# Attention and feed-forward in one kernel: the projected K transposed by DMA, V projected onto both partition halves, and the first stages reordered

## Chip, cores, metric

One core of one Trainium2 chip. The metric is the device time of one execution in microseconds (us), given as the median of several. A profiled execution has a span (first to last instruction) about 1.8 us shorter than its device time (518.4 against 520.21 us before). Executions of one kernel here scatter by 0.4 to 5 us, which is as much as the effects under study, so below I also use an interval inside a profile that repeated to 0.01 us in three profiles of the change.

## The reference

```python
# q, k, v: (8 batches, 8 heads, 1024 tokens, 64); E, F: (64, 1024)
k_proj = np.einsum('ks,bhsd->bhkd', E, k)
v_proj = np.einsum('ks,bhsd->bhkd', F, v)
scores = np.matmul(q, k_proj.transpose(0, 1, 3, 2)) / np.sqrt(64)
attn = softmax(scores)                       # over the 64 projected keys
x = np.matmul(attn, v_proj)                  # -> (8192 tokens, 512)
h = np.maximum(x @ w_in, 0.0)                # w_in: 512 x 2048
out = h * h @ w_out                          # w_out: 2048 x 512, f32 out
```

## The kernel before

Everything runs in bf16 with f32 sums. GpSimd's queue loads and casts (f32 to bf16). TensorE's order is fixed by hand. The feed-forward part (FFN) of batch b goes in 64 numbered *steps*, each of four 128x512 matmuls (0.86 us), and `at(step, stage)` puts the attention stages of the next batches between them. Batches are counted from 0 here. "Second batch" is batch 1. LO and HI are partitions 0 to 63 and 64 to 127. A PSUM bank holds the sums of TensorE until another engine has copied them out. A *slot* is the time from the start of one matmul to the start of the next.

```python
def load(t, src):                         # all loads but E
    return nc.gpsimd.dma_start(t, src)
...
for g in range(2):                        # batch 0, in two halves of four heads
    load(K0[:, half[g]], tokens(k, 0, h=half[g]))
    load(Q0[:, half[g], 0:4, :], tokens(q, 0, h=half[g], i=slice(0, 4)))
    if g == 0:
        make_identity(nc, ident[:])
load(f_bf[:], F[:])
for g in range(2):
    load(V0[:, half[g]], tokens(v, 0, h=half[g]))
... # then w_in, w_out (with the second half of Q0 before its last piece), K, V, Q of batch 1, 2, ...

def project(self):                        # K and V of one batch, in pairs of matmuls
    ps = bank()                           # one of four PSUM banks, shared with the FFN
    for i in range(NI):
        nc.tensor.matmul(ps[LO, :], lhsT=ET[:, i, :], rhs=self.K[:, :, i, :], ...)
        nc.tensor.matmul(ps[HI, :], lhsT=FT[:, i, :], rhs=self.V[:, :, i, :], ...)
    self.keep_k(ps[LO, :])                # two VectorE copies 64x512 into kp
    self.keep_v(ps[HI, :])                # ScalarE and VectorE copies into both halves of vp

def transpose_k(self, h=slice(0, 8)):
    ps = bank([P, H, KP], BF16)
    for hh in range(h.start, h.stop):     # eight transposes, 64 rows -> 64 columns
        nc.tensor.transpose(ps[:, hh, :], self.kp[:, hh].rearrange("k a d -> k (a d)"), ident[0:KP, 0:KP])
    nc.vector.tensor_copy(self.kT[:, h], ps[:, h])

def transpose_q_dma(self):                # Q is transposed by DMA from batch 2 on
    nc.sync.dma_start_transpose(self.qT[...], self.Q[...])
... # plan
at(36, nxt.project); at(37, nxt.transpose_q, 0); at(37, nxt.transpose_q, 1)   # batch 1, during batch 0
at(61, coming.project); at(64, coming.transpose_k)                            # batch 2, during batch 0
at(30, coming.project); at(49, coming.transpose_k)                            # later batches
```

The softmax here doesn't subtract the row's maximum and nothing guards it: scores larger than these inputs give would overflow.

## Time and profile before

| | before |
|---|---|
| median (lowest to highest) | 519.8 us (519.7 to 520.09) |
| TensorE busy | 507.5 of 518.4 us |
| a batch in the steady part (same place, next batch) | 61.18 us |
| 128x512 matmuls, start to start | 0.216 us |

The page of the profile before: the span, busy time and share of each engine, then 40 slices of the span with busy tenths, granted TensorE clock in tenths and the share of the DMA engines.

```profile
span 518.4 us, 6881 instructions
...
PE 507.5 (98%) x2774; PEld 224.2 (43%) x2774; DVE 175.7 (34%) x369; ACT 286.1 (55%) x426; POOL 31.9 (6%) x44
...
PE   7899999999999999999999999999999999999997
...
PEclk8999999999999999999999999999999999999999
DMA  9999999899997299204831050110101011010102
```

TensorE has work in every slice; DMA is at nine tenths in thirteen of the first sixteen slices and falls away later. Whether those first slices are limited by one or the other cannot be read from shares, so next comes the chain of work that ended last in the profile before (start, duration, what).

```profile
14.31 16.57 DMA w_in_122<-in_moe_w_in_dram
31.17 30.68 DMA Q_sb<-in_q_dram
61.90 1.07 PE ps_bank L227 x16
```

The chain is a DMA chain until 61.9 us: the load of the second batch's Q, issued at 31.17 us behind megabytes of weights, K and V, lands at 61.85 us, and TensorE's transposes of it (L227) follow at once. From there on the chain is TensorE. The waits of TensorE before (who waited for what: us in total, times, longest):

```profile
PE ps_bank L328 <- DVE xT L311: 1.1, 2, 0.9
PE ps_bank L207 <- ACT kp L172: 0.8, 1, 0.8
PE ps_bank L183 <- ACT o_sb L341: 0.6, 1, 0.6
...
PE ps_bank L227 <- DMA Q_sb<-in_q_dram: 0.6, 1, 0.6
```

L227 waited 0.6 us for Q. So at that point TensorE was the earlier of the two, but only just.

Two places where K is transposed, from the timeline of TensorE before (start, duration, instruction, count). First the block at step 49 of a steady batch, then the one of the second batch:

```profile
140.89 1.03 PE L334 MATMUL ps_bank<-w_out_124,hsq 128*128 128x512 bf16 x4
141.85 0.41 PE L248 MATMUL ps_att<-expT,ones 64*64 64x512 bf16 x4
142.09 0.39 PE L282 MATMUL ps_att<-expT,vp 64*64 64x512 bf16 x4
142.41 0.40 PE L207 MATMUL ps_bank<-ident,kp 64*128 64x64 bf16 x8
142.75 1.04 PE L334 MATMUL ps_bank<-w_out_126,hsq 128*128 128x512 bf16 x4
```

```profile
62.80 1.89 PE L328 MATMUL ps_bank<-xT,w_in_118 128*128 128x512 bf16 x8
64.62 0.40 PE L207 MATMUL ps_bank<-ident,kp 64*128 64x64 bf16 x8
64.96 1.04 PE L328 MATMUL ps_bank<-xT,w_in_118 128*128 128x512 bf16 x4
```

A durations column cannot be added up here, as matmuls overlap; starts can. Four matmuls of 0.216 us from 140.89 end their slots at 141.75, and the next FFN matmul starts at 142.75: a gap of 1.00 us for L248, L282 and the K transposes L207. In the second block, eight slots from 62.80 end at 64.53 and the next FFN matmul starts at 64.96: 0.43 us for the K transposes alone.

### The profile page before, as it was taken

To read this page: it belongs to the slowest core of one execution; us is meant where nothing else is said; L and a number is where in the kernel's file an instruction comes from. 1 tells how busy PE (TensorE), PEld (TensorE's weight loads), DVE (VectorE), ACT (ScalarE), POOL (GpSimd) and SP (SyncE) were. 2 spreads that over 40 slices of the span, in tenths; PEclk is the share of its full clock that TensorE was granted. 3 is DMA by queue.
4 is the path that set the end of the run, shared out by engine and by line. 5 is a ranking of instruction groups with operands and counts; after the bars stand their busy time and mean duration, and the time that the engine had idled before them with its cause. 6 is when DMAs were issued, how large, how long until landed. Compare 5 with 4: busy or idle time off the path is not lost.

```text
span 518.4 us, 6881 instructions
## 1 busy us (share of the span) xinstructions
PE 507.5 (98%) x2774; PEld 224.2 (43%) x2774; DVE 175.7 (34%) x369; ACT 286.1 (55%) x426; POOL 31.9 (6%) x44
## 2 busy tenths in 40 slices
PE   7899999999999999999999999999999999999997
PEld 3444443444444444444444444444444444444443
DVE  2451552433514154041532335132440424323130
ACT  1475476566626756276654747356672766544351
POOL 6430100120100020000100000000000000000000
PEclk8999999999999999999999999999999999999999
DMA  9999999899997299204831050110101011010102
GB/s 149 204 205 214 234 207 184 133 219 195 200 186 140 61 177 170 82 0 122 148 78 61 1 142 21 42 41 21 61 1 61 21 40 42 20 62 20 62 0 81
DMA packets 64975, 53.26 MB, mean 103 GB/s; under 512 B 26416, under 2 KB 56624, under 8 KB 64944
## 3 DMA queue, kind: packets, MB, share of 16 engines
q0 software_dynamic: 30880, 29.49, 36.0%
q1 hardware_dynamic: 34064, 23.34, 15.8%
q8 instruction: 21, 0.34, 0.3%
q14 instruction: 10, 0.08, 0.0%
HBM read 59.24 MB, written 16.78 MB: 147 GB/s over the span
## 4 chain that ended last, share of the span: by engine, by line
PE 87%; DMA 11%; POOL 1%; issue 0%; ACT 0%; POOLq 0%
PE ps_bank L334 40%; PE ps_bank L328 39%; DMA Q_sb<-in_q_dram 8%; DMA w_in_122<-in_moe_w_in_dram 3%; PE ps_bank L183 2%; PE ps_att L248 2%; PE ps_att L242 1%; PE ps_bank L282 1%; PE ps_att L282 1%; PE ps_bank L207 0%; PE ps_bank L227 0%; POOL K_sb L76 0%; ACT o_sb L341 0%; ACT rs L261 0%; POOL Q_sb L76 0%
## 5 line engine op out<-in xcount | busy, mean ns | idle before, releaser
L324 ACT ACTIVATE h_relu<-ps_bank 128x512 bf16<-128x512 f32 x256 | 151.1, 598 | 69.4 <-PE ps_bank L328 68.6
L325 DVE TENSOR_TENSOR hsq<-h_relu 128x512 bf16<-128x512 bf16 x256 | 108.7, 425 | 193.9 <-ACT h_relu L324 192.9
L334 PEld LDWEIGHTS <-hsq 128*128 128x128 bf16 x1024 | 97.5, 98 | 123.8 <-issue 10.1
L341 ACT COPY o_sb<-ps_bank 128x512 f32<-128x512 f32 x64 | 37.4, 586 | 112.9 <-PE ps_bank L334 112.9
L334 PE MATMUL ps_bank<-w_out_128,hsq 128*128 128x512 bf16 x256 | 65.7, 380 | 0.0
L334 PE MATMUL ps_bank<-w_out_124,hsq 128*128 128x512 bf16 x256 | 65.6, 379 | 0.0
L334 PE MATMUL ps_bank<-w_out_126,hsq 128*128 128x512 bf16 x256 | 65.5, 379 | 0.0
L334 PE MATMUL ps_bank<-w_out_131,hsq 128*128 128x512 bf16 x256 | 65.4, 379 | 0.0
L328 PE MATMUL ps_bank<-xT,w_in_122 128*128 128x512 bf16 x256 | 59.1, 379 | 0.0
L328 PE MATMUL ps_bank<-xT,w_in_118 128*128 128x512 bf16 x256 | 58.2, 379 | 0.0
L328 PE MATMUL ps_bank<-xT,w_in_120 128*128 128x512 bf16 x256 | 58.2, 379 | 0.0
L261 ACT ACTIVATE rs<-ps_att 128x1024 f32<-128x1024 f32 x32 | 32.7, 1025 | 24.6 <-PE ps_att L248 24.6
L286 DVE TENSOR_TENSOR xT<-ps_bank,rs 128x512 bf16<-128x512 f32 x30 | 19.3, 686 | 60.2 <-ACT rs L262 60.2
L328 PEld LDWEIGHTS <-w_in_122 128*128 128x128 bf16 x256 | 24.5, 98 | 31.4 <-issue 2.9
L328 PEld LDWEIGHTS <-w_in_120 128*128 128x128 bf16 x256 | 24.9, 98 | 30.1 <-issue 0.4
L328 PEld LDWEIGHTS <-w_in_118 128*128 128x128 bf16 x256 | 24.8, 98 | 30.0 <-issue 0.4
L256 ACT ACTIVATE expT<-ps_att 128x1024 bf16<-128x1024 f32 x32 | 31.8, 1023 | 8.0 <-PE ps_att L242 8.0
L262 ACT ACTIVATE rs<-rs 128x1024 f32<-128x1024 f32 x32 | 33.8, 1059 | 0.5
L328 PE MATMUL ps_bank<-xT,w_in_114 128*128 128x512 bf16 x128 | 30.6, 379 | 1.1 <-DVE xT L311 1.1
L328 PE MATMUL ps_bank<-xT,w_in_116 128*128 128x512 bf16 x128 | 30.4, 379 | 0.0
L286 DVE TENSOR_TENSOR xT<-ps_att,rs 128x512 bf16<-128x512 f32 x26 | 16.8, 687 | 33.0 <-ACT rs L262 33.0
L328 PEld LDWEIGHTS <-w_in_114 128*128 128x128 bf16 x128 | 12.3, 98 | 16.1 <-issue 1.7
(65 smaller groups left out, 205.2 us busy)
## 6 DMA issues: line engine op xcount, KB each, us to landing
out_dram<-o_sb SPq DMA_DIRECT2D x64, 256.0 KB, 2.0
K_sb<-in_k_dram POOLq DMA_DIRECT2D x7, 1024.0 KB, 18.4
V_sb<-in_v_dram POOLq DMA_DIRECT2D x7, 1024.0 KB, 24.3
Q_sb<-in_q_dram POOLq DMA_DIRECT2D x7, 1024.0 KB, 12.5
K_sb<-in_k_dram POOLq DMA_DIRECT2D x2, 512.0 KB, 8.5
V_sb<-in_v_dram POOLq DMA_DIRECT2D x2, 512.0 KB, 12.6
Q_sb<-in_q_dram POOLq DMA_DIRECT2D x2, 256.0 KB, 8.9
w_in_118<-in_moe_w_in_dram POOLq DMA_DIRECT2D x1, 512.0 KB, 15.6
```

Of the source, the lines that this page charges most:

```text
L183: nc.tensor.matmul(ps[LO, :], lhsT=ET[:, i, :], rhs=self.K[:, :, i, :], start=f, stop=l)
L248: nc.tensor.matmul(ps[o, par], lhsT=ones[r, :], rhs=e[r, par], start=True, stop=True)
L256: nc.scalar.activation(e[:], ps[:], AF.Exp, scale=SCALE)
L261: nc.scalar.activation(rs[:], ps[:], AF.Ln)
L262: nc.scalar.activation(rs[:], rs[:], AF.Exp, scale=-1.0)
L282: nc.tensor.matmul(ps_x[par][o], lhsT=self.vp[r, 2 * pr + a, :], rhs=e[r, par], start=True, stop=True)
L286: nc.vector.tensor_tensor(out=self.xT[:, pr, :, par], in0=ps_x[par].rearrange("p (c t) -> p c t", c=2), in1=rs[:, par].rearrange("p (c t) ...
L324: nc.scalar.activation(r[:], ps[:], AF.Relu)
L325: nc.vector.tensor_tensor(out=self.hsq[c][:, fb, :], in0=r[:], in1=r[:], op=ALU.mult)
L328: nc.tensor.matmul(ps[:], lhsT=w_in_blk(cb, fb), rhs=self.xT[:, cb, c].rearrange("p a t -> p (a t)"), start=(cb == 0), stop=(cb == NCB - 1),)
L334: nc.tensor.matmul(ps[:], lhsT=self.hsq[c][:, fb, tb * P:(tb + 1) * P], rhs=w_out_blk(fb), start=(fb == 0), stop=(fb == NFB - 1),)
L341: nc.scalar.copy(o[:], ps[:])
```

## The change

The intent: take the K transposes off TensorE by letting the DMA do them (from batch 3 on), pair heads so that the remaining TensorE transposes are four of 128 columns and not eight of 64, and shorten the prologue (batch 0): F earlier, V projected onto both halves by paired matmuls so that one 128-row copy does, a copy moved off ScalarE, stages in another order. The very last output block is done in two halves.

```diff
@@ loads of batch 0
         if g == 0:
             make_identity(nc, ident[:])
-    load(f_bf[:], F[:])
+            load(f_bf[:], F[:])
@@ layout of projected K: heads j and j+4 share a 128-row block
-            self.kp = proj_pool.tile([KP, H, 2, D], BF16, name="kp")
-            self.kT = proj_pool.tile([P, H, KP], BF16, name="kT")
+            self.kp = proj_pool.tile([P, H // 2, 2, D], BF16, name="kp")
+            self.kT = proj_pool.tile([P, H // 2, 2, KP], BF16, name="kT")
@@ project
-            self.keep_k(ps[LO, :])
+            for g in range(2):                       # four 64x256 copies instead of two 64x512
+                self.keep_k(ps[LO, g * C // 2:(g + 1) * C // 2], g)
@@ project_v (batch 0)
-                nc.tensor.matmul(ps[HI, 0:C // 2], lhsT=FT[:, i, :], ...)
-            self.keep_v(ps[HI, 0:C // 2], half[g], nc.vector.tensor_copy)
+                for o in (LO, HI):
+                    nc.tensor.matmul(ps[o, 0:C // 2], lhsT=FT[:, i, :], ...)
+            nc.vector.tensor_copy(self.vp[:, half[g]], ps[:, 0:C // 2]...)
@@ transposes of K
+            for j in range(H // 2):
+                nc.tensor.transpose(ps[:, j, g, :]..., self.kp[rows, j]..., ident[rows, rows])
+        def transpose_k_dma(self):
+            nc.sync.dma_start_transpose(self.kT[...], self.kp[...])
@@ last block of the last batch
+                        if last and tb == 3:
+                            for m in (slice(0, DM // 2), slice(DM // 2, DM)):
+                                ps = bank()
+                                for fb in range(NFB):
+                                    self.second_mm(c, tb, fb, ps, m)
+                                self.store(c, tb, ps, m)
@@ prologue order (cut) and plan
-        warm(2)
+        FT = projection("FT", f_bf)
         att.project_k(1)
@@
-                at(2, att.chunk_values, 0, 1)
+                at(1, att.chunk_values, 0, 1)
@@
-                        at(49, coming.transpose_k)
+                        at(31, coming.transpose_k_dma)
```

More of the change, by code (lines that the diff above doesn't have):

```diff
@@ L165, in load, with keep_k, keep_v @@
             return first
-        def keep_k(self, ps_k, h=slice(0, 8), second=None):
+        def keep_k(self, ps_k, g, second=None):
             view = ps_k.rearrange("k (h d) -> k h d", d=D)
-            nc.vector.tensor_copy(self.kp[:, h, 0, :], view)
-            (second or nc.vector.tensor_copy)(self.kp[:, h, 1, :], view)
-        def keep_v(self, ps_v, h=slice(0, 8), first=None):
+            rows = (LO, HI)[g]
+            nc.vector.tensor_copy(self.kp[rows, :, 0, :], view)
+            (second or nc.vector.tensor_copy)(self.kp[rows, :, 1, :], view)
+        def keep_v(self, ps_v):
             view = ps_v.rearrange("k (h d) -> k h d", d=D)
-            (first or nc.scalar.copy)(self.vp[HI, h], view)
-            nc.vector.tensor_copy(self.vp[LO, h], view)
+            nc.scalar.copy(self.vp[HI], view)
+            nc.vector.tensor_copy(self.vp[LO], view)
         def project(self):
@@ L193, in project_k @@
                 )
-            self.keep_k(ps[LO, 0:C // 2], half[g], nc.scalar.copy)
+            self.keep_k(ps[LO, 0:C // 2], g, nc.scalar.copy if g == 0 else None)
         def project_v(self, g):
@@ L198, in project_v, with transpose_k @@
             for i in range(NI):
-                nc.tensor.matmul(
-                    ps[HI, 0:C // 2], lhsT=FT[:, i, :], rhs=V0[:, half[g], i, :], start=(i == 0), stop=(i == NI - 1)
-                )
-            self.keep_v(ps[HI, 0:C // 2], half[g], nc.vector.tensor_copy)
-        def transpose_k(self, h=slice(0, 8)):
-            ps = bank([P, H, KP], BF16)
-            for hh in range(h.start, h.stop):
-                nc.tensor.transpose(
-                    ps[:, hh, :], self.kp[:, hh].rearrange("k a d -> k (a d)"), ident[0:KP, 0:KP]
-                )
-            nc.vector.tensor_copy(self.kT[:, h], ps[:, h])
+                for o in (LO, HI):
+                    nc.tensor.matmul(
+                        ps[o, 0:C // 2], lhsT=FT[:, i, :], rhs=V0[:, half[g], i, :],
+                        start=(i == 0), stop=(i == NI - 1),
+                    )
+            nc.vector.tensor_copy(self.vp[:, half[g]], ps[:, 0:C // 2].rearrange("k (h d) -> k h d", d=D))
+        def transpose_k(self, gs=(0, 1)):
+            ps = bank([P, H // 2, 2, KP], BF16)
+            rows = slice((LO, HI)[gs[0]].start, (LO, HI)[gs[-1]].stop)
+            g = slice(gs[0], gs[-1] + 1)
+            for j in range(H // 2):
+                nc.tensor.transpose(
+                    ps[:, j, g, :].rearrange("p g k -> p (g k)"),
+                    self.kp[rows, j].rearrange("k a d -> k (a d)"), ident[rows, rows]
+                )
+            nc.vector.tensor_copy(self.kT[:, :, g], ps[:, :, g])
+        def transpose_k_dma(self):
+            nc.sync.dma_start_transpose(
+                self.kT[:].rearrange("p j g k -> p j (g k)"), self.kp[:].rearrange("p j a d -> p (j a d)")
+            )
         def transpose_q_chunk(self, c, src, hg):
@@ L242, in scores_mm @@
                 nc.tensor.matmul(
-                    ps[o, par], lhsT=self.kT[r, h, :], rhs=self.qT[r, h, n, :], start=True, stop=True
+                    ps[o, par], lhsT=self.kT[r, h % 4, h // 4, :], rhs=self.qT[r, h, n, :], start=True, stop=True
                 )
@@ L331, in first_mm, with second_mm, store @@
             )
-        def second_mm(self, c, tb, fb, ps):
+        def second_mm(self, c, tb, fb, ps, m=slice(0, DM)):
             nc.tensor.matmul(
-                ps[:], lhsT=self.hsq[c][:, fb, tb * P:(tb + 1) * P], rhs=w_out_blk(fb),
+                ps[:, m], lhsT=self.hsq[c][:, fb, tb * P:(tb + 1) * P], rhs=w_out_blk(fb)[:, m],
                 start=(fb == 0), stop=(fb == NFB - 1),
             )
-        def store(self, c, tb, ps):
+        def store(self, c, tb, ps, m=slice(0, DM)):
             o = out_pool.tile([P, DM], F32, name="o_sb")
-            nc.scalar.copy(o[:], ps[:])
+            nc.scalar.copy(o[:, m], ps[:, m])
             i = 2 * (2 * c + tb % 2) + tb // 2
-            nc.sync.dma_start(out_rows[self.b, i, :, :], o[:])
+            nc.sync.dma_start(out_rows[self.b, i, :, m], o[:, m])
         def steps(self):
@@ L378, in steps @@
                 else:
+                    last = self.b == B - 1 and c == 1
                     for tb in range(4):
+                        if last and tb == 3:
[4 more added lines that the diff above has]
+                                self.store(c, tb, ps, m)
+                            break
                         ps = bank()
@@ L396 @@
         att.transpose_q_chunk(0, Q0, 0)
-        att.transpose_k(half[0])
+        att.transpose_k((0,))
         warm(1)
         att.chunk_scores(0, 0)
-        warm(2)
+        FT = projection("FT", f_bf)
         att.project_k(1)
@@ L403 @@
         att.transpose_q_chunk(0, Q0, 1)
-        att.transpose_k(half[1])
-        warm(1)
-        att.chunk_scores(0, 1)
-        FT = projection("FT", f_bf)
-        warm(3)
-        att.chunk_sums(0, 1)
-        att.project_v(0)
-        warm(2)
+        att.transpose_k((1,))
+        warm(2)
+        att.chunk_scores(0, 1)
+        warm(4)
+        att.project_v(0)
+        att.chunk_sums(0, 1)
+        warm(1)
         att.chunk_values(0, 0)
-        warm(2)
+        warm(1)
         att.project_v(1)
```

## The prediction

> **What bounds the kernel now.** The page shows TensorE busy for 507.5 of 518.4 us at a granted clock of 1.00 after the start, so from about 62 us on the time is a sum of TensorE slots: 128x512 matmuls start every 0.216 us (timeline), and a batch takes 61.18 us without any TensorE wait in the view of waits.
> Before 62 us the limit is DMA: the chain of waits is a DMA chain up to 61.85 us, when the second batch's Q lands; TensorE waits 0.57 us for it (L227). From 31.2 to 61.85 us about 11 MB are read (1 MB per w_out piece, 2 MB each for K, V, Q), an estimate of 358 GB/s from those sizes. The Trainium skill, "DMA: Bandwidth & Descriptors", section "Bandwidth", names about 358 GB/s as the HBM limit of a core; the trace agrees.
>
> **What the change does.**
> 1. *K transposed by DMA, five times (batches 3 to 7, counted from 0).* Each removes eight TensorE transposes. Around step 49 the gap between FFN matmuls is 1.00 us with them (141.75 to 142.75) and 0.65 us where there are none (445.81 to 446.46): 0.34 us each, on the critical path. 5 x 0.34 = -1.7 us. The 0.43 us VectorE copies that go are off it. Q's DMA transpose, eight times larger, took 4.1 us alone and 20 us beside loads (L234); K's I estimate at 0.5 to 3 us. It has from step 31 to step 14 of the next batch, about 40 us: hidden.
> 2. *Batches 1, 2 and the halves of batch 0:* four 128-column transposes for eight 64-column ones: about 0.
> 3. *Copies out of the K projection:* four 64x256 (0.42 us) instead of two 64x512 (0.67 us), 0.2 to 0.3 us longer. The projection's bank is now free 0.3 us before TensorE wants it again (129.36 against 129.67 us): 0 to 0.1 us of wait per batch, +0.1 us in all.
> 4. *Prologue:* F earlier, V projected onto both halves (pairs run together, like L183/L184), one 128-row copy instead of two, values a step earlier, second K copy off ScalarE (0.8 us at L207). FFN should start at about 21.6 instead of 22.6 us and the 1.1 us stall on xT near 25 us mostly vanish: 2 us gained by 28 us. But DMA gets no faster: the second half of Q0 lands at about 41.2 us (TensorE now asks at 41.6), the next Q at about 61.9 us. TensorE gets there early and waits. Net about 0.
> 5. *Tail:* the last block in halves: last copy 0.36 instead of 0.59 us, a shorter final store, but 256-column matmuls are spaced 0.113 rather than 0.108 us. About -0.3 us.
>
> Sum: -1.7 + 0.1 + 0 - 0.3 = -1.9 us: **517.9 us, range 516.3 to 519.4**. Faster by over 2%: 0.01; within 2%: 0.98; slower: 0.01.
>
> **What would show it.** FFN matmuls start near 21.6 us; a new wait of 1 to 1.6 us on Q near 40 us; the wait on the second Q grows from 0.57 to about 1 us, ending at 61.5 to 62.2; the rest shortens by about 1.9 us; steady batches take 60.8 to 60.9 us; nobody waits for K's DMA transposes.
>
> **What would make it wrong.** If the Q load lands earlier, the prologue's 2 us come through (about 516). If K's transpose holds up stores behind it in its queue, or the longer copies hold a bank, batches gain less or lose.

## The result

| | before | after |
|---|---|---|
| median (lowest to highest), 4 runs each | 519.79 us (519.7 to 520.09) | 516.57 us (516.2 to 517.81) |
| ratio (95% interval) | | 0.9941 (0.9923 to 0.9959) |
| span of the profiled run | 518.4 us | 514.5 us |
| TensorE transposes of the second batch's Q start | 61.90 us | 60.32 us |
| from there to the last ScalarE copy | 452.97 us | 450.94 us |

Ratios are the mean time of one kernel's fast runs over that of the other's of the same rounds, so not quite the ratio of the medians. The time fell by about 3.1 us, within the range of the prediction but more than its 1.9. Two later measurements of the same pair gave ratios of 0.9953 (0.9927 to 0.9979) and 0.9938 (0.9917 to 0.9959). The page after:

```profile
span 514.5 us, 6878 instructions
...
PE 505.2 (98%) x2756; PEld 224.1 (44%) x2756; DVE 174.2 (34%) x377; ACT 285.4 (55%) x426; POOL 31.8 (6%) x44
...
PE   7999999999999999999999999999999999999997
...
PEclk9999999999999999999999999999999999999999
DMA  9999999999996399106941051100101011010102
```

The chain that ended last, after:

```profile
12.02 17.02 DMA w_in_122<-in_moe_w_in_dram
...
29.33 30.94 DMA Q_sb<-in_q_dram
60.32 1.07 PE ps_bank L241 x16
```

It has the same form, but the Q load was issued at 29.33 and landed at 60.27 us, 1.58 us earlier than in the profile before. The other 2.3 us of the difference in span (518.4 - 61.90 against 514.5 - 60.32) lie behind that point. The waits of TensorE after:

```profile
PE ps_bank L241 <- DMA Q_sb<-in_q_dram: 1.1, 1, 1.1
PE ps_bank L231 <- DMA Q_sb<-in_q_dram: 0.7, 2, 0.4
PE ps_bank L185 <- ACT o_sb L355: 0.6, 1, 0.6
...
PE ps_bank L342 <- DVE xT L325: 0.2, 1, 0.2
```

The waits for Q have grown, as forecast: 1.1 us at the second batch (L241) and a new one of 0.4 us at the second half of Q0, which together with a 0.3 us wait in the prologue makes the 0.7 of L231. The stall on xT is down from 1.1 to 0.2 us. The two places where K was transposed, after:

```profile
138.88 1.03 PE L348 MATMUL ps_bank<-w_out_124,hsq 128*128 128x512 bf16 x4
139.83 0.41 PE L262 MATMUL ps_att<-expT,ones 64*64 64x512 bf16 x4
140.07 0.39 PE L296 MATMUL ps_att<-expT,vp 64*64 64x512 bf16 x4
140.39 1.04 PE L348 MATMUL ps_bank<-w_out_126,hsq 128*128 128x512 bf16 x4
```

```profile
61.22 1.89 PE L342 MATMUL ps_bank<-xT,w_in_118 128*128 128x512 bf16 x8
62.95 0.39 PE L215 MATMUL ps_bank<-ident,kp 128*128 128x128 bf16 x4
63.17 1.03 PE L342 MATMUL ps_bank<-xT,w_in_118 128*128 128x512 bf16 x4
```

At step 49 four slots from 138.88 end at 139.74 and the next FFN matmul starts at 140.39: a gap of 0.65 us, exactly the one forecast for a batch without K transposes. The second batch's block (eight slots from 61.22 end at 62.95, next FFN matmul at 63.17) costs 0.22 instead of 0.43 us: that was not forecast. K's own DMA transpose, from the view of the tile kT after (durations are shortest, median and longest in ns):

```profile
L222 SPq DMA_TRANSPOSE kT<-kp x5: 1231/1234/1652, 137.7 to 369.7; - x5
...
who waited for it (us, times):
...
  PE ps_att L256: 0.6, 2
...
DMA to landing us min/median/max: 2.3/2.9/11.1
```

Five transposes of 128x512 took 1.23 to 1.65 us of queue time and landed after 2.3 to 11.1 us. The two that took over 10 us were issued about 2 us after a batch's K and V loads. The TensorE waits for kT are 0.6 us in two pieces, which the view of waits puts down to the VectorE copies of the prologue; none is for a DMA. Nobody waited for K's DMA transposes.

So three things were open: why the second Q landed 1.58 us earlier, whether K's part is only TensorE slots, and what the prologue is worth.

### The profile page after: what moved, and what is told of

Read it like the earlier page. It is cut to its first block, busy times and chain, and to the rows that moved or that the text cites. A ratio compares the mean times of both kernels' runs of the same rounds, so it can differ in the third digit from the quotient of the medians.

```text
span 514.5 us, 6878 instructions
## 1 busy us (share of the span) xinstructions
PE 505.2 (98%) x2756; PEld 224.1 (44%) x2756; DVE 174.2 (34%) x377; ACT 285.4 (55%) x426; POOL 31.8 (6%) x44
## 4 chain that ended last, share of the span: by engine, by line
PE 87%; DMA 11%; issue 1%; ACT 0%; POOL 0%; POOLq 0%; ACTq 0%
PE ps_bank L348 41%; PE ps_bank L342 40%; DMA Q_sb<-in_q_dram 6%; DMA w_in_122<-in_moe_w_in_dram 3%; PE ps_bank L185 2%; PE ps_att L262 2%; DMA K_sb<-in_k_dram 2%; PE ps_att L256 1%; PE ps_bank L296 1%; PE ps_att L296 1%; PE ps_bank L241 0%; ACT rs L275 0%; ACT o_sb L355 0%; POOL K_sb L76 0%; POOL f_bf L76 0%
## 5 line engine op out<-in xcount | busy, mean ns | idle before, releaser
L348 PEld LDWEIGHTS <-hsq 128*128 128x128 bf16 x1040 | 99.0, 98 | 124.3 <-issue 10.1
L355 ACT COPY o_sb<-ps_bank 128x512 f32<-128x512 f32 (+1 forms) x65 | 37.5, 579 | 110.8 <-PE ps_bank L348 110.8
L348 PE MATMUL ps_bank<-w_out_128,hsq 128*128 128x512 bf16 (+1 forms) x260 | 65.9, 376 | 0.0
L348 PE MATMUL ps_bank<-w_out_124,hsq 128*128 128x512 bf16 (+1 forms) x260 | 65.8, 376 | 0.0
L348 PE MATMUL ps_bank<-w_out_126,hsq 128*128 128x512 bf16 (+1 forms) x260 | 65.6, 376 | 0.0
L348 PE MATMUL ps_bank<-w_out_131,hsq 128*128 128x512 bf16 (+1 forms) x260 | 65.6, 376 | 0.0
L275 ACT ACTIVATE rs<-ps_att 128x1024 f32<-128x1024 f32 x32 | 32.7, 1024 | 27.3 <-PE ps_att L262 27.3
L270 ACT ACTIVATE expT<-ps_att 128x1024 bf16<-128x1024 f32 x32 | 31.9, 1024 | 8.6 <-PE ps_att L256 8.6
## 6 DMA issues: line engine op xcount, KB each, us to landing
V_sb<-in_v_dram POOLq DMA_DIRECT2D x2, 512.0 KB, 11.1
```

The costliest lines, as they stand in the source:

```text
L270: nc.scalar.activation(e[:], ps[:], AF.Exp, scale=SCALE)
L275: nc.scalar.activation(rs[:], ps[:], AF.Ln)
L348: nc.tensor.matmul(ps[:, m], lhsT=self.hsq[c][:, fb, tb * P:(tb + 1) * P], rhs=w_out_blk(fb)[:, m], start=(fb == 0), stop=(fb == NFB - 1),)
L355: nc.scalar.copy(o[:, m], ps[:, m])
```

## The experiments

All outputs are right. The table has each profiled run; "prologue" says whose stages before the FFN it has. The last column is the interval from the first transpose of the second batch's Q to the start of the last ScalarE copy. A late start of the loads does not touch it; in e2, e8 and e10 it is 0.14 to 0.26 us longer than in their like, for a reason that I did not look for. In e5, e6, e8, e10 and e12 the profile shows no wait for K before the first projection, so there the third column is TensorE's start and not the landing.

| run | prologue | first projection matmul | second Q's transposes | wait for it | Q to last copy |
|---|---|---|---|---|---|
| before | old | 8.52 | 61.90 | 0.57 | 452.97 |
| e1_before_F_early | old, F early | 9.04 | 61.67 | none | 452.97 |
| e4_K_dma_only | old | 7.19 | 60.62 | 0.58 | 450.86 |
| after | new | 6.98 | 60.32 | 1.08 | 450.94 |
| e3_after_again | new | 9.02 | 62.33 | 0.78 | 450.94 |
| e12_after_third | new | 7.26 | 60.51 | 0.99 | 450.94 |
| e5_after_K_on_PE | new | 7.39 | 60.38 | 1.19 | 452.06 |
| e6_after_no_tail | new | 7.25 | 60.66 | 1.30 | 450.85 |
| e2_after_F_late | new, F late | 7.22 | 61.53 | none | 451.08 |
| e8_before_Q_later | old | 7.45 | 61.85 * | none | 451.50 * |
| e10_Q_later_old_prologue | old | 7.52 | 63.48 * | none | 449.44 * |
| e7_after_Q_later | new | 7.22 | 61.38 * | none | 449.20 * |
| e11_Q_later_again | new | 7.33 | 61.00 * | 0.27 ** | 449.21 * |
| e9_Q_and_project_later | new | 7.16 | 60.76 * | 0.26 ** | 448.50 * |

\* With Q's transposes two steps (1.73 us) later; add 1.73 to the last column to compare.

\*\* Not in the view of waits, which counts from the modelled end of the matmul before, about 0.17 us after the end of its slot. In e11 twelve slots from 58.14 end at 60.73, Q lands at 60.95 and the transposes start at 61.00; in e9 the three times are 60.50, 60.71 and 60.76.

### Why the load stream was earlier: e1, e2, e3

e1 is the kernel before with F loaded early, e2 the change with F loaded late, e3 the change itself. They shared a chip and 11 runs of before (median 518.96 us, 518.69 to 523.15).

```diff
# e1 (before):                          # e2 (after): the reverse
         if g == 0:
             make_identity(nc, ident[:])
-    load(f_bf[:], F[:])
+            load(f_bf[:], F[:])
```

> The kernel before with one edit: F is loaded right after Q's first half, as in the change. Open: in the profile of the change the load stream ran about 1.6 us earlier than in that of before (first half of K landed near 7.0 instead of 8.5 us, the second batch's Q at 60.3 instead of 61.85 us). Theory ORDER (the place of F among the first loads makes the stream earlier): first K half lands near 7.0 us, second Q near 60.3 us, time 518.2 to 518.8 us in every run. Theory CHANCE (the start of the stream differs from execution to execution whatever the kernel): either landing may appear in the profile, and the times scatter over about 1.5 us, between 518.2 and 519.9. Theory OTHER (the earlier stream comes from something else in the change, such as what TensorE or VectorE do early): landings as before, 519.7 us.

Measured: 519.2 us median (518.95 to 519.97), ratio 0.9996 (0.9969 to 1.0022).

> The change with one edit undone: F is loaded after Q's second half again. TensorE will then wait for F near 12 us, which the wait for the second Q should swallow. ORDER: first K half lands near 8.5 us, second Q near 61.9 us, time 517.8 to 518.1 us in every run. CHANCE: times scatter over 1.5 us as those of the change do (516.2 to 517.8), landing either way. OTHER: landings as in the change (60.3 us), time 516.3 to 516.6 us.

Measured: 517.31 us (516.64 to 517.89), ratio 0.9958 (0.9934 to 0.9983).

> The change once more, for the scatter of its times (516.2, 516.3, 516.8, 517.8 so far, against 519.7 to 520.1 of before). ORDER: nearly all runs near 516.3 us, the 517.8 an outlier. CHANCE: times spread between 516.2 and 517.9 in several runs of each, perhaps in two groups 1.5 us apart; a profile with a late landing (61.8 us) would go with about 517.8.

Measured: 516.81 us (516.35 to 518.3), ratio 0.9953 (0.9927 to 0.9979). The profiled run was its slowest, 518.3 us.

From the timeline of TensorE in e1 (F early), the first K projection and the second Q's transposes; the bracket, where there is one, is idle time before and what ended it:

```profile
9.04 1.87 PE L191 MATMUL ps_bank<-K_sb,ET 128*64 128x256 bf16 x8 [1.74 <-DMA K_sb<-in_k_dram]
...
61.67 1.06 PE L227 MATMUL ps_bank<-ident,Q_sb 128*128 128x128 bf16 x16
```

And the same two lines in e3, which is the change itself:

```profile
9.02 1.87 PE L194 MATMUL ps_bank<-K_sb,ET 128*64 128x256 bf16 x8 [2.36 <-DMA K_sb<-in_k_dram]
...
62.33 1.07 PE L241 MATMUL ps_bank<-ident,Q_sb 128*128 128x128 bf16 x16 [0.78 <-DMA Q_sb<-in_q_dram]
```

The theory ORDER falls: with F early the first K half landed near 9 us twice, with F late it landed near 7.2 us twice. The very same kernel landed it at 7.0 us in the profile of the result and at 9.0 us here. This is CHANCE: the start of the load stream differs between executions of one kernel by 2 us, and where TensorE waits for the second Q, the whole run moves with it. In before, after, e3 and e4 the transposes of the second Q began 53.3 to 53.4 us after the first K projection, whichever kernel it was. So the 1.58 us earlier landing in the profile of the result need not be an effect of the change. Two things stay open. Late starts (8.5 us or more) are in two of five profiles with the old prologue and in one of nine with the new, too few to say whether they are as likely in both. And the start is not all: the second Q landed 52.9 to 53.6 us after the first K projection in eleven profiles, but 51.3 us after it in e1 and e10 and 52.5 in e2.

e1's second line shows something else: there was no wait for Q at all. There TensorE came last, 1.35 us after Q had landed at 60.32 us. e1's prologue is that of before but for the place of F. So I read before as standing at the edge, limited by the loads in one execution and by its own prologue in another; a second profile of before itself was not taken. e2's expected time missed: it showed neither 517.8 to 518.1 in every run nor 516.3 to 516.6. Its TensorE waited 3.1 us for F, and the time rose by only 0.5 us against e3: most of that was swallowed by the waits for Q, which are gone in it.

### K's part alone: e4 and e5

e4 is before with the paired layout, the four copies and the DMA transpose; e5 is the change with TensorE transposes in every batch.

```diff
# e4: change without F early, new stage order, new V projection, tail halves
# e5:
-                        at(31, coming.transpose_k_dma)
+                        at(49, coming.transpose_k)
```

> The kernel before with K's part of the change alone: paired layout of the projected K, four copies, DMA transpose from the fourth batch on; loads, stage order, V projection and tail as before. My sum: five slots of 0.34 us gone, batches of 60.84 instead of 61.18 us, time 518.1 us (517.9 to 518.3), second Q landing as before at 61.85 us if the landing is not a matter of chance. If K's DMA transpose or the longer copies cost anything on the path, the batches keep more than 60.9 us.

Measured: 518.17 us (516.85 to 521.74), ratio 0.9984 (0.995 to 1.0018). As a time this is inconclusive, the runs spread over 5 us. Inside the profile it is clear: 450.86 against 452.97 us, 2.11 us less.

> The change with K transposed by TensorE in every batch again (four 128-column transposes at step 49 in the new paired layout); all else as in the change. Chance in the start of the load stream moves a whole run by up to 2 us, so I measure from the first Q transpose of the second batch to the start of the last ScalarE copy: 452.97 us before, 450.94 us in the change (both repeated to 0.01 us). My theory (TensorE slots alone): a block of four transposes costs 0.22 us, so five of them bring 450.94 + 1.1 = 452.0 us, batches of 61.06 us. Rival (the DMA transpose also freed something else, such as a PSUM bank or VectorE): the whole 1.7 us comes back, 452.6 us. Time near 517.9 us, give or take the chance.

Measured: 517.26 us (one run, so its state is unknown); 452.06 us in the interval, against 450.94 of the change: +1.12 us. From the timeline of TensorE in e5, step 49:

```profile
138.94 1.03 PE L348 MATMUL ps_bank<-w_out,hsq 128*128 128x512 bf16 x4
139.90 0.41 PE L262 MATMUL ps_att<-expT,ones 64*64 64x512 bf16 x4
140.14 0.39 PE L296 MATMUL ps_att<-expT,vp 64*64 64x512 bf16 x4
140.46 0.40 PE L215 MATMUL ps_bank<-ident,kp 128*128 128x128 bf16 x4
140.69 5.56 PE L348 MATMUL ps_bank<-w_out,hsq 128*128 128x512 bf16 x25
```

Four slots from 138.94 end at 139.80; the next FFN matmul starts at 140.69: a gap of 0.89 us, 0.24 more than the 0.65 without K transposes (L215 to the next FFN matmul: 0.23). Five of these are the 1.1 us. That the whole 1.7 us would come back, the rival, is excluded. K's part therefore has two terms: 5 x 0.34 us for the eight narrow transposes that are gone, and 2 x 0.21 us in batches 1 and 2, where four wide ones replace eight narrow ones. Together 2.12 us, which is e4's 2.11.

### The tail alone: e6

```diff
-                    last = self.b == B - 1 and c == 1
+                    last = False
```

> The change with the last block of the last batch in one piece again. From the first Q transpose of the second batch to the start of the last copy: 450.86 us (0.08 less than the change, whose 256-column matmuls are a little slower), and from there to the end of the span 3.5 to 3.7 us instead of 3.24. If the halves were worth more than 0.2 to 0.4 us, the sum grows by more than that.

Measured: 517.04 us (one run, so its state is unknown). The last copy starts at 450.85 us in the interval, as expected 0.09 earlier than with halves; from there to the end of the span it is 3.8 us (515.3 - 511.51), against 3.2 in the change (514.5 - 511.26) and 3.5 before (518.4 - 514.87). The halves are worth 0.2 to 0.5 us by these pairs. Over all fourteen profiles this last stretch is 3.1 to 3.3 us with the halves (nine) and 3.5 to 3.8 without (five); the means differ by 0.42, so about 0.3 us is left after the 0.09.

### What the prologue is worth: e7, e8, e10, e11, e12

If the new prologue's gain went into waits for Q, then moving the stages that need Q later must bring it out.

```diff
# e7 and e11 (on the change), e8 (on the kernel before)
-                at(20, att.transpose_q_chunk, 1, Q0, 0)        # and hg = 1
+                at(21, att.transpose_q_chunk, 1, Q0, 0)        # chunk_scores 22 -> 23, chunk_sums 25 -> 26
-                    at(37, nxt.transpose_q, 0)                 # and 1
+                    at(39, nxt.transpose_q, 0)
# transpose_k 39 -> 40, scores 41 -> 42, transpose_q 2 and 3 43 -> 44, values 45 -> 46
# e10: the same on the change, with the prologue of before
```

> The change with the stages that need late loads moved later: transposes of the second half of the first Q and what follows by one step, those of the second batch's Q by two steps (the rest of that batch's early stages by one). Theory ABSORBED (the new prologue is about 1.5 us faster for TensorE but all of it turned into waits for Q): those waits, 0.37 and 1.08 us, shrink below 0.3 us in sum and the time falls by 1.0 to 1.5 us against the change, to about 515.5 us. Rival: the load stream then sets the time elsewhere (another load, or the batch's later stages wait), less than 0.4 us gained.

Measured: 515.02 us (514.9 to 515.59); before beside it 518.88 us (518.44 to 519.63); ratio 0.9926 (0.9912 to 0.9939).

> The kernel before with the same move of stages. ABSORBED: before has only its 0.57 us wait for Q to gain, so 0.3 to 0.6 us less than before; the difference between this run and the change moved likewise is then 2.3 us plus 1.0 to 1.5 us of prologue, 3.3 to 3.8 us. Rival: both gain alike, difference 2.3 us.

Measured: 519.56 us (518.68 to 520.01), ratio 1.001 (0.9997 to 1.0022). Before gained nothing, where I had expected 0.3 to 0.6 us. The difference between the two is 4.5 us by the medians and not 3.3 to 3.8. e8's five runs lie in two groups, 518.7 to 518.9 and 519.6 to 520.0 us; its profile is of the faster one, and what slows the other was not looked at.

> The same move of stages with K's part and the tail of the change, but with the prologue of before (F late, V on one half and two copies, stages in the old order). It tells what the prologue alone is worth once the waits for Q are out of the way. ABSORBED: 1.5 to 2.1 us slower than the run with the new prologue, about 516.8 us. Rival (the prologue is worth nothing in itself): within 0.4 us of it.

Measured: 517.76 us (515.77 to 517.93), ratio 0.9953 (0.9928 to 0.9979).

> The change with the stages moved later, once more, so that it is measured beside the change itself on one chip. 515.0 us (514.7 to 515.6), that is 1.4 to 1.8 us less than the change beside it.

Measured: 515.18 us (514.84 to 516.52), ratio 0.9917 (0.9895 to 0.9939).

> The change a third time, beside the others: 516.4 to 516.9 us median. If its median is more than 2.6 us under that of before, the load stream's start is better than chance in it; if it is 2.1 to 2.5 us under, the prologue brings nothing on average and K, the four-column-block transposes and the tail are all.

Measured: 516.45 us (516.32 to 517.14), ratio 0.9938. Before, in the same rounds as e9 to e12, had 519.71 us (518.54 to 522.06). That is 3.3 us by the medians, so by the rule set beforehand the load stream's start would be better than chance in the change. I do not take that as shown: before's runs spread over 3.5 us here, the fastest of the two kernels differ by 2.2 us (518.54 against 516.32), and no profile of before was taken in these rounds.

The waits of TensorE in e12 (the change) and in e11 (the same with the stages later), from one chip:

```profile
PE ps_bank L241 <- DMA Q_sb<-in_q_dram: 1.0, 1, 1.0
PE ps_bank L342 <- DMA w_in<-in_moe_w_in_dram: 1.0, 1, 1.0
PE ps_bank L231 <- DMA Q_sb<-in_q_dram: 0.9, 1, 0.9
```

```profile
PE ps_bank L185 <- ACT o_sb L355: 0.6, 1, 0.6
...
PE ps_bank L231 <- DMA Q_sb<-in_q_dram: 0.3, 1, 0.3
PE ps_bank L348 <- DMA w_out<-in_moe_w_out_dram: 0.2, 1, 0.2
```

In e12 TensorE waited 1.0 and 0.9 us for the two late parts of Q, and before that 1.0 us for the first piece of w_in: there the new prologue ran into the loads already at the start of the FFN (20.59 us). In e11 the waits for Q that the view lists are down to the 0.3 us of the prologue, with 0.2 us for a weight; the 0.27 us before the second Q's transposes (see the table) comes on top, so this version stands at the edge of the loads. e11 is 1.3 us faster than e12 (515.18 against 516.45, a little less than the 1.4 to 1.8 expected): the gain of the prologue is there and was turned into waits. ABSORBED holds, and its rival falls. On the old prologue the move brings nothing, and with the old prologue under the move (e10) the kernel is slower than with the new one: by 2.6 us by the medians (517.76 against 515.18), by 1.9 us by the ratios, as one of e10's six runs took 515.77 us. So the rival that the prologue is worth nothing in itself falls too; whether it is worth more than the 1.5 to 2.1 us that I had expected there is not settled.

Part of this difference can be seen in e10's timeline of TensorE: two identical groups, the projections of the two halves of V.

```profile
18.46 1.91 PE L202 MATMUL ps_bank<-V_sb,FT 128*64 128x256 bf16 x8
...
22.21 1.06 PE L202 MATMUL ps_bank<-V_sb,FT 128*64 128x256 bf16 x8
```

The first group of eight took 1.91 us, the second 1.06. The Trainium skill ("TensorE: Matmul & The Clock Gate", Part 1, "What's actually happening") says that TensorE runs at half rate until its activity has filled a free-running window of about 3.4 us and that where the change falls differs from run to run. The trace agrees as to half rate and scatter: the first K projection took 1.03 us in the profile of the change and 1.92 us in e12, the same kernel. e10's granted clock was 0.70 between 15 and 20 us; e12's reads 1.00 where its slow group ran, so the clock record is not to be trusted at this scale, which the same page warns of ("Seeing it yourself"). A ramp at the start alone does not explain why a slow group can follow a fast one; that stays open here: in e10 the second K projection had taken 1.06 us at 12.18 us, before the slow group at 18.46. A prologue that has no spare time before the second Q pays for such a phase; the new one has about 1.5 us to spare (the waits of 0.37 and 1.08 us in the profile of the result). Whether the old prologue meets such phases more often, I did not test: five of e10's six runs lie near 517.8 and one at 515.77 us.

### A version that beats both: e9

The remaining 0.64 us wait for a PSUM bank at the third batch's projection was in every run with that stage at step 61.

```diff
# e9: e7 and
-                        at(61, coming.project)
+                        at(62, coming.project)
-                        at(64, coming.transpose_k)
# and in the plan of the next batch
+                    if b == 1:
+                        at(2, nxt.transpose_k)
```

> The change with the late loads' stages moved (515.0 us when run alone) and, besides, the third batch's K and V projection one step later, with its K transposes at step 2 of the next batch. Aim: the 0.64 us that TensorE waits there for a PSUM bank that ScalarE still copies out of, in every run so far. Theory BANK: that wait goes, about 0.6 us less, 514.4 us. Rival: the wait moves to the next user of a bank, 515.0 us.

Measured: 514.3 us (514.11 to 514.76), ratio to before 0.9896 (0.9875 to 0.9916), beside e11's 515.18. The wait at the projection is gone from the list of waits and the interval is 448.50 against 449.21 us: BANK holds. This version is 5.4 us (1.0%) under before, by the ratio, and 2.15 us under the change.

## Why the prediction was right or wrong

- **The bound: right.** DMA to the landing of the second Q, TensorE from there. The interval after it is the same to 0.01 us in three profiles of the change. The 358 GB/s took 1 MB as a million bytes; a piece is 1024 KB in f32 (512 KB after the cast), and eleven of them in 30.68 us are 376 GB/s (an estimate).
- **K by DMA, -1.7 us: right.** The gap at step 49 is 0.65 us as forecast, the steady batch 60.84 us (125.23 to 186.07, against 127.24 to 188.42 before). The DMA transpose landed in 2.3 to 11.1 us, beyond the estimate of 0.5 to 3 us in two cases of five, and was hidden either way.
- **"Four 128-column transposes for eight 64-column ones: about 0": wrong**, the step that failed in the mechanism: the cost was taken to go with the columns. Counting columns (512 each) I took them for equal. The block cost 0.43 us before and 0.22 after, twice, and e4 and e5 both close with it: -0.4 us.
- **Longer copies, +0.1 us: a little too much.** No wait appeared. In batch 1 the bank came free at 127.57 us and TensorE wanted it at 127.65 (an estimate, three slots of 0.863 us after 125.06): the margin shrank from 0.31 to 0.08 us and held.
- **Tail, -0.3 us: right**, 0.2 to 0.5 by e6.
- **Prologue, "net about 0": mechanism right, sizes too large, the net not settled.** The waits for Q grew as forecast. FFN matmuls started at 20.85 us (forecast 21.6), but most of that is the earlier load stream, which is luck: counted from the first K projection they started only 0.22 us earlier than before (13.87 against 14.09 us), where 1.0 was forecast, and the matmuls of the third piece of w_in 1.1 us earlier (18.22 against 19.31), where 2 was forecast. In this pair of profiles the waits took all of it: the second Q's transposes began 53.34 against 53.38 us after the first K projection. But the sum needed is an average over executions, and I had read the wait of 0.57 us in one profile as if before always waited there. e1 had none, and e10's TensorE would have come to that point only at 61.75 us (63.48 - 1.73), with Q landed at 58.83: in such executions the old prologue is itself the limit, and the new one gains. Taking the 2.3 us behind the second Q from the three measured differences (by ratio 3.1, 2.4 and 3.2 us) leaves 0.1 to 0.9 us for it. Each of the three is uncertain by about 1 us, and the fastest runs of the two later rounds differ by 2.3 and 2.2 us, which leaves nothing; so this gain is argued and not shown.
- **The sum.** Forecast -1.9, measured -2.4 to -3.2 us. The mis-sized terms are the wide transposes (0 against -0.4), the copies (+0.1 against 0) and perhaps the prologue (0 against at most -0.9). The earlier landing in the profile, which the prediction named as the thing that would bring 516 us, did occur; the change's own profiles show it with and without, so I count it as chance.

## What to carry to other kernels

A stage can lose a gain to a later wait without any trace of it in the total; read how long the engine already waits there, and expect that number to vary between executions before building a sum on it. When a gain was absorbed, move the consumer of the late load behind other work: here that brought 1.3 us back for an edit of step numbers. Where start-up scatter is as large as the effect, compare intervals that begin after the scatter; they repeated to 0.01 us in three profiles of one kernel, where the totals spread over 1 to 5. And before comparing start times of two profiles, take off what the load stream's own start has moved.

## What the Trainium skill lacked or had wrong

- "TensorE: Matmul & The Clock Gate", "Back-to-back issue gap", gives about 131 ns per matmul of 512 columns as sustained in a real stream and calls 216 ns the isolated gap. Here a sustained stream with a weight load for every matmul keeps 216 ns (16 in 3.45 us), the number that Part 1 of the same page gives for a warm array.
- The same page, Part 4, gives durations of one 128x128 transpose (about 390 ns alone, 275 ns in a kernel). In a row they cost far less than that: 16 in 0.90 us, 0.056 us each. Besides the floors for small matmuls in Part 1, it has no figure for a row of narrow transposes, which are dearer than their columns: eight of 64 columns on 64 rows took 0.43 us between FFN matmuls, four of 128 columns 0.22 us. Why was not tested.
- No page has a time from issue to landing for a small DMA transpose inside SBUF that runs beside loads (this would belong in "DMA: Bandwidth & Descriptors"). Here 128x512 bf16 took 1.23 to 1.65 us of queue time and 2.3 to 11.1 us to land (median 2.9).
- No page that I read says that the first load of a kernel lands at different times: 7.0 to 9.0 us for the same kernel here, which shifted the whole run where it was bound by loads.
